# Attention into a top-1 mixture of experts: order of norms, evacuations and turned products around expert 0 and 1

## The chip, the cores and the metric

One core of a Trainium2 chip runs the whole program in one launch. The metric is the device time of an execution in microseconds. A run's profile is one more execution, taken with the hardware profiler.

## The reference

The reference is a causal attention with a learned decay (8 batches of 8 heads, 576 positions, head size 64), followed by a mixture of 8 experts over the 4608 resulting rows of 512. Each row goes to the one expert whose embedding has the largest cosine with it, and is weighted with that expert's softmax probability.

```python
scores = scale * q @ k.T + minimum(-(cum[:, None] - cum[None, :]), 0)   # causal
x = softmax(scores) @ v                       # heads side by side: 4608 x 512
logits = normalised(x) @ normalised(expert_emb).T / tau
expert_idx = argmax(logits)
out[row] = softmax(logits)[expert_idx] * (relu(x[row] @ w1[expert_idx]) @ w2[expert_idx])
```

## The kernel before

Precision is kept with pairs of 16-bit tiles, a high part and a remainder; each product of two such values is three products on the tensor engine (high by high, high by remainder, remainder by high).

**Attention.** `step(n)` (L968) is one step of a pipeline over the 64 heads, with `NH` = 64. In step n the engines do the score products and exponentials of head n, the weighted sums (`pv`, L495) of head n-2 and the norm (`norm1` to `norm3`, L515 to L541) of head n-3. All heads use one accumulator `om`, so the sums of a head wait until the norm of the head before has read it: norm of head 62, then sums of head 63. Steps 64, 65 and 66 have no new head; they finish the sums and norms of heads 62 and 63 and already start expert 0. For that, `tail(n)` (L1118) is called ahead of the sums: in steps 64 to 66 it runs `l1(0)`, `l1(1)`, `l1(2)` (L1139).

**Expert 0's first layer.** `l1(m, e, lo, hi)` (L838) computes block m of the hidden layer (128 of 1024 features) in 12 products into a buffer of PSUM, of which these blocks have two, and then evacuates it with `hsplit` (L834): ScalarE writes the relu as the high part, the vector engine subtracts it for the remainder. Blocks 3 to 7 follow after the last step (L1169).

**Weights.** They arrive by DMA in pieces of 128x512 floats. `wsq` (L790) squares a piece on ScalarE for the norm, `wnorm` (L794) turns the sums into a scale (with a small product on the tensor engine that shares `om`), `wcv` (L805) writes the high half on ScalarE and puts the remainder on a list, and `wlow` (L818) works the list off on the vector engine (L821) and lets the sync queue issue the load of a later piece. In the steps, `wcv` holds the remainders for the `wlow` of the next step (L1039). Pieces 3 and 4 of the first weights lie in the buffer that block 0's evacuated output takes.

**Routing.** When the norm of a batch's last head is done, `router` (L580) queues small vector steps (sum, maximum, comparison, one-hot `oh`, ranks). They run in `slots` and `some` (L1141). Rows are then scattered by expert in DRAM (L652) and gathered again tile by tile with `xload` (L708). `xprep(e, t)` (L725) turns a gathered tile of 128 rows around: for experts 0 and 1 with four transposes on the tensor engine, a copy on ScalarE (L750) and a subtraction on the vector engine (L752), for later experts with two transposing DMAs (L739 to L742). `xstat` (L716) takes its statistics.

**The tail.** An expert has room for 640 rows: four groups of 128, and a tail of 64 that is always computed and 64 more that run only if the expert has over 576 rows (`tc.If`, L859 and L880). The tail is computed turned around: the first layer of all eight blocks goes to one PSUM tile `T`, `l1tail` (L858) splits it, `turned` (L874) multiplies it into `yT` (12 products for a block), `l2tail` (L879) copies `yT` to SBUF on ScalarE (L884), and `l2tail_out` (L886) transposes it into `Y` and scales it out. `yT` and `Y` are the two halves of one PSUM tile (L853), a bank each, and `Y` also serves as a transposing buffer for `xprep(1, 0)` and `xprep(1, 3)`.

**Second layer.** `l2(e, t, mid)` (L901) computes group t of the output: eight times three products into one accumulator, with `mid[m]` called after block m, then `put` (L914), which scales the result on the vector engine (L917) and scatters it to the output (L918).

**The order** is written out by hand: each engine runs its instructions in the order in which the program issues them, and waits only on what it reads or overwrites.

- Expert 0's end: two rounds of tail products (L1214 to L1221), each with an `hsplit`, an `xprep` and an `xload`; then `l1tail(0)`; then `l2(0, 3)`, with `turned(0, 0)` to `turned(0, 5)` after its blocks 2 to 7, `xprep(1, 3)` and two conversions after block 1, and `xprep(1, 4)` after block 7; then `put`, two conversions, the last two turned blocks, two conversions (L1229 to L1237).
- Expert 1's end (loop over t): group 0, group 1 with its turned products, then at t = 2 the `xprep(2, 4)`, the norm, three conversions, two squares and then `l2tail(1)`; at t = 3 group 2, which calls `l2tail_out(1)` after its block 3.

Of the kernel before, what the change touches and what calls it, by code (L numbers as in the profile page):

```python
# [43 lines left out]
SPL = 384  # L44
NBIG = 1 << 20
MAIN = 512
# [63 lines left out]
def main(ctx, tc, qkh, qkc, vtin, s_in, emb, tau, w1h, w2h, out, shared, nb):  # L110
# [557 lines left out]
    X, WT, HT = {}, {}, {}  # L668
# [85 lines left out]
    def pxm():  # L754
        return ps_m.tile([128, 512], F32, tag="m", name="pxm")
# [78 lines left out]
    def hsplit(hH, hL, hp):  # L834
        nc.scalar.activation(hH, hp, AF.Relu)
        nc.vector.scalar_tensor_tensor(hL, hp, 0.0, hH, op0=ALU.max, op1=ALU.subtract)

    def l1(m, e, lo, hi, mid=None):  # L838
        h = pxs()[:, 0:hi - lo] if e else ps_t.tile([128, 2, 512], F32, tag="t", name="h")[:, 0, 0:hi - lo]
        l1mm(h, m, e, lo, hi, mid, e > 0)  # L840
        hsplit(*(t[:, lo:hi] for t in htile(m)), h)

    def four(t):
        return t.rearrange("p (m t) -> p m t", m=4)
# [78 lines left out]

    tasks, scats, mq, aq = deque(), deque(), deque(), deque()
    sent = []
    late, rq, first, placed, brk = deque(), deque(), deque(), [], [False]

    def soon(*fs):
        tasks.extendleft(reversed(fs))
# [38 lines left out]
    def step(n):  # L968
        m = n + LA - (n < 1)
        live = 0 <= n < NH  # L970
        b0, b1, c8 = n // H, n // H + 1, n % H
        prev = 0 <= n - 1 < NH
        g, c = n // HG, n % HG
        if m == 0:
            rsetup()
            load(0)
            hset(0)
            for i in range(2):
                for f in (neg, hcopy):
                    f(0, True, i)  # L980
                    f(0, False, i)
                addl(0, True, pair(i))
                addl(0, False, pair(i))
                if i == 0:
                    load(1)
                    zeros(1)
                    loadc(1)
            setup2()
            zeros(2)
        if n < 0 and rq:  # L990
            rq.popleft()()
            aq.popleft()()
            for p in range(2):
                loadt(0, pair(p))
        if m == 2:
            setup3()
        if m == 3:
            r7s[0]()
        if live and c == 0:
            hset(g + 1)  # L1000
            if n > 0:
                load(g + 2)
                loadc(g + 2)
        fslot()
        norm1(n - 3)
        if live:
            ta_(n)
        if not live or n < 2:
            s1(m)
        if n < 0:  # L1010
            heat(1)
        if prev:
            pl_(n - 1, 576, PS(n), "p")
        if n == 1:
            load(2)
        sr(m, 3)
        norm2(n - 3)
        (sa if n > 1 else s2)(m)
        if n < 0:
            heat(1)  # L1020
        if live:
            expa(n)
            if n != 1:
                prep(n, True)
        norm3(n - 3)
        if live:
            tb_(n)
        sr(m, 2)
        if n < 2:
            sr(m, 1)  # L1030
        s3(m)
        if n < 0:
            heat(2)
        if live:
            tbl(n)
        mslot()
        if prev and PS(n) < 1600:
            pl_(n - 1, PS(n), 1600, "v")
        wlow()  # L1039
        k = n - NH + 8  # L1040
        if k > 7:
            wsq((12, 14, 16)[k - 8])
        if n == 1:
            vscale(0)
            fslot()
            while tasks:
                slot()
            emm(0)
            s1(LA)
            s2(LA)  # L1050
            for i in (3, 2, 1):
                sr(LA, i)
            vcp(0, False)
            vcp(0, True)
            prep(1, True)
            s3(LA)
            emm(1)
            s4(LA)
            mrow1(LA)
        if live and n > 1:  # L1060
            emm(n)
        if n > 1:
            sb(m)
            sbr(m)
        tail(n)
        pv(n - 2, [0, 1, 2])
        if rq:
            rq.popleft()()
        if n < 2:
            s4(m)  # L1070
        if n < 0:
            heat(2)
        if n == NH - 1:
            xprep(0, 2, pxs(), False)
        pv(n - 2, [3, 4])
        if live:
            expb1(n)
            if n:
                vcp(n, False)
            else:  # L1080
                vsq(0, range(4))
        aslot()
        if n == 0:
            nc.sync.dma_start(cumd.rearrange("x r s -> r x s").bitcast(F32), chl.bitcast(F32))
            loadc(2)
            setup4()
        if live:
            prep(n, False)
            if n:
                vcp(n, True)  # L1090
        if k > 0:
            wsq((0, 2, 3, 6, 8, 8, 9, 10, 12, 14, 16)[k])
            wcv((0, 0, 0, 0, 0, 1, 2, 2, 1, 2, 0)[k], True)
        brk[0] = False
        slots(4)
        if live and 2 <= c8 < 6 and b1 < nb:
            vsq(b1, (c8 - 2,))
        if live and c8 == 6 and b1 < nb:
            vscale(b1)
        if live and c8 < 4:  # L1100
            loadt(b1, c8)
        if n == NH - 8:
            wissue(3)
        for _ in range(SCN[c8] if n < NH - 22 else 1 + (c8 > 5) + 4 * (n > NH - 6)):
            scatter()
        later()
        if live and c == (n < HG):
            addl(g + 1, True)
        if live and c == 1:
            addl(g + 1, False)  # L1110
        mrow1(m)
        if live:
            pl_(n, 0, 576, "p")
# [4 lines left out]
    def tail(n):  # L1118
        k = n - NH + 8
        if k in (2, 3):  # L1120
            wissue(7 + k % 2)
        if k == 3:
            later()
            while len(placed) < 5 * (nb - 2):
                scatter()
        if k == 4:
            HT["Kx"] = const.tile([128, 4, DM], F32, tag="KC0", name="Kx")
            HT["Qx"] = const.tile([128, 3 * XR + DM], F32, tag="QC0", name="Qx")
            wissue(16)
            xinfo(0, 0, SPL // 128)  # L1130
        if k == 5:
            wnorm()
            for t in range(3):
                xload(0, t)
        if k == 7:
            for t in range(2):
                xprep(0, t, pxs(), False)
        if 8 <= k < 11:
            l1(k - 8, 0, 0, SPL)  # L1139

    def some(k):  # L1141
        mslot()
# [23 lines left out]

    for n in range(1 - LA, NH + 3):
        step(n)
    for m in range(3, 8):  # L1169
        l1(m, 0, 0, SPL, partial(some, 12) if m == 5 else wnorm if m == 4 else None)  # L1170
        if m == 3:
            wlow()
            some(12)
        if m > 3:
            wcv((2, 1, 2, 2)[m - 4])
        if m < 6:
            xstat(0, m - 3)
        if m > 5:
            some(0)
        if m == 7:  # L1180
            for f in X[("g", 0, 0)][0:2]:
                f()
# [31 lines left out]
    for i in range(2):  # L1214
        hb = four(pxs())
        for m in range(4 * i, 4 * i + 4):
            l1mm(hb[:, m % 4], m, 0, SPL, MAIN, tail=True)
        hsplit(*(X[("T", 1)][:, k, 4 * i:4 * i + 4] for k in range(2)), hb)
        xprep(1, i, (HT["Y"], pxm())[i])
        xload(1, 3 + i)  # L1220
        gate3.popleft()()  # L1221
    l1tail(0)
    gate3.popleft()()

    def convert():
        wnorm()
        wcv(2)

    def last():  # L1229
        turned(0, 5, 0)  # L1230
        xprep(1, 4, pxm())
    mids = {m: partial(turned, 0, m - 2, 0) for m in range(2, 7)}
    l2(0, 3, {**mids, 1: lambda: (xprep(1, 3, HT["Y"]), convert()), 7: last})
    wcv(2)
    for m in (6, 7):
        turned(0, m, 0)
    wcv(2)  # L1237
    for e in range(1, NE):
        nx = e + 1 < NE
        w2, w1 = 16 * e + 8, 16 * e + 16  # L1240
        for m in range(8):
            l1(m, e, 0, MAIN)
            if e == 1 and m < 2:
                (l2tail, l2tail_out)[m](0)
            if m == 2:
# [35 lines left out]
                shared["total"] = nc.values_load(shared["ci"][0:1, NE - 1:NE], min_val=0, max_val=NT // 128)  # L1281
        l1tail(e)
        for t in range(NTL):
            if nx:
                if t + 2 < NTL:
                    xprep(e + 1, t + 2)
                if e == 1 and t < 2:
                    wsq(w1 + 6 + 2 * t)
                if t == 1 + (e == 1):
                    wnorm()  # L1290
                if t:
                    wcv(2 if e > 1 else (0, 0, 3, 3, 2)[t])
                if e > 1 or t > 1:
                    wsq(w2 + 16 + min(8, 2 * t + 2 if e > 1 else 3 * t - 4))
                if t == 4 and e > 1:
                    wnorm()
            if t == 4:
                (l2 if nx else l2h)(e, LAST)
            elif t == 3:
                l2(e, 2, {3: partial(l2tail_out, e)})  # L1300
            elif t == 2:
                l2tail(e)
            else:
                l2(e, t, tail=(t == 1))

# [123 lines left out]
```

## Time and profile before

| | |
|---|---|
| median of 3 runs | 790.51 us (788.7 to 792.61) |
| the profiled execution's own time | 788.63 us |
| span from its first to its last instruction | 786.9 us |
| tensor engine (PE) busy | 753.7 us, 96% of the span |
| vector engine (DVE) / ScalarE (ACT) / GpSimd (POOL) busy | 525.4 / 569.8 / 383.2 us |
| granted clock of the tensor engine, mean | 0.993 |

The span is the time between the first and last recorded instruction of one execution; its own time also holds the start and end around it. Times in the rows are microseconds from the span's start. A row of the timeline has start, length, engine, line, operation, output<-input, shapes and count (equal neighbours are merged, and products overlap, so lengths can reach beyond the next start); in brackets stands how long the engine was idle before it, and what released it.

### The profile page before, as it was taken

How to read it: one execution, taken by the hardware profiler on the slowest of the kernel's cores; microseconds unless marked ns; L12 is line 12 of the kernel's file. 1: busy time of each engine (PE TensorE's matmuls, PEld its weight loads, DVE VectorE, ACT ScalarE, POOL GpSimd, SP SyncE). 2: the span in 40 equal slices, each digit the busy share in tenths (PEclk: the TensorE clock that was granted, in tenths of full speed). 3: DMA queues.
4: the chain of work that ended last, by engine and by line, in shares of the span. 5: the costliest groups of instructions: out<-in, count | busy, mean ns of one | idle time of the engine just before them, and what ended most of it. 6: DMA issues, size and time to landing. Idle time of an engine off the chain costs nothing. (4 is left out here: it accounts for less than half of the span.)

```text
span 786.9 us, 22460 instructions
## 1 busy us (share of the span) xinstructions
PE 753.7 (96%) x8765; PEld 552.5 (70%) x8765; DVE 525.4 (67%) x1788; ACT 569.8 (72%) x1020; POOL 383.2 (49%) x370
## 2 busy tenths in 40 slices
PE   8799999999999999987989989999999999999997
PEld 3699999999999999984465545655645555556564
DVE  7767888888888878867656856556555566655611
ACT  6699989898999988975845876837738578475410
POOL 8767798989898979762432212130131211311001
PEclk9899999999999999999999999999999999999999
DMA  8997879797989886770634875546755857644001
GB/s 156 194 207 136 176 172 215 169 217 171 207 180 204 186 194 152 182 257 37 206 113 138 203 185 168 131 151 168 144 195 118 191 174 162 206 118 99 15 15 55
DMA packets 76914, 125.33 MB, mean 159 GB/s; under 512 B 38960, under 2 KB 39364, under 8 KB 75934
## 3 DMA queue, kind: packets, MB, share of 16 engines
q0 software_dynamic: 20240, 70.92, 38.8%
q1 hardware_dynamic: 56560, 52.84, 25.7%
q8 instruction: 76, 1.25, 0.7%
q14 instruction: 38, 0.31, 0.1%
HBM read 95.23 MB, written 21.49 MB: 148 GB/s over the span
## 5 line engine op out<-in xcount | busy, mean ns | idle before, releaser
L240 POOL TENSOR_TENSOR PL<-P 128x576 f16<-128x576 f32 (+2 forms) x128 | 203.3, 1693 | 19.5 <-ACT P L483 10.9
L830 PEld LDWEIGHTS <-wt 128*128 128x128 f16 x2016 | 114.9, 98 | 90.0 <-issue 4.6
L830 PE MATMUL pxs<-xH,wt 128*128 128x512 f16 (+1 forms) x512 | 149.8, 360 | 0.2 <-PEq L880 0.2
L918 POOL DMA_INDIRECT out<-Kx,xj x39 | 41.9, 1075 | 180.1 <-DVE Kx L917 164.5
L511 PE MATMUL om<-vh,P 128*128 128x73 f16 x960 | 106.9, 199 | 5.1 <-DVE xt L536 4.4
L512 PE MATMUL om<-vl,P 128*128 128x72 f16 x960 | 106.3, 196 | 0.0
L513 PE MATMUL om<-vh,PL 128*128 128x73 f16 x960 | 106.1, 198 | 0.0
L830 PE MATMUL T<-xH,wt 128*128 128x64 f16 x768 | 105.9, 193 | 0.0
L712 POOL DMA_INDIRECT Qx<-xs,idx x40 | 41.9, 1047 | 129.2 <-ACT vjunk L785 75.8
L348 PE MATMUL s<-qkb 96*128 96x288 f32 (+4 forms) x270 | 96.9, 372 | 2.6 <-DVE M L356 1.1
L512 PEld LDWEIGHTS <-P 128*128 128x128 bf16 x960 | 94.8, 99 | 6.2 <-issue 5.8
L513 PEld LDWEIGHTS <-PL 128*128 128x128 f16 x960 | 93.8, 98 | 0.0
L511 PEld LDWEIGHTS <-P 128*128 128x128 bf16 x960 | 93.7, 98 | 0.2
L830 PE MATMUL pxs<-xL,wt 128*128 128x512 f16 (+1 forms) x256 | 92.1, 360 | 0.0
L356 DVE CUSTOM_DVE_ANT_0 junk<-s,mS 128x320 bf16<-128x320 f32 (+3 forms) x142 | 73.2, 523 | 5.8 <-PE s L348 4.3
L905 PE MATMUL pxs<-wt,hp 128*128 128x512 f16 x270 | 73.0, 379 | 0.0
L905 PE MATMUL pxs<-wt,hq 128*128 128x512 f16 x270 | 69.4, 379 | 0.0
L486 ACT ACTIVATE P<-tb 128x1024 f32<-128x1024 f32 x64 | 65.1, 1018 | 3.2 <-PE tb L453 1.5
L917 DVE TENSOR_SCALAR Kx<-pxs,xj,idx 128x512 f32<-128x512 f32 x31 | 25.1, 808 | 59.7 <-PE pxs L905 46.2
L450 PE MATMUL tb<-QC,KC 128*128 128x448 f32 (+3 forms) x256 | 64.0, 309 | 0.0
L821 DVE SCALAR_TENSOR_TENSOR wt<-ring,idx,wt 128x512 f16<-128x512 f32 x80 | 56.9, 747 | 9.4 <-ACT wt L813 8.9
L483 ACT ACTIVATE P<-ta 128x576 f32<-128x576 f32 x64 | 41.2, 643 | 29.7 <-PE ta L450 28.0
(270 smaller groups left out, 1984.1 us busy)
## 6 DMA issues: line engine op xcount, KB each, us to landing
qkb<-qkh POOLq DMA_DIRECT2D x15, 1216.0 KB
ring<-w2h SPq DMA_DIRECT2D x44, 256.0 KB
ring<-w1h SPq DMA_DIRECT2D x36, 256.0 KB
vT<-vtin SPq DMA_DIRECT2D x28, 320.0 KB
KC<-qkh POOLq DMA_DIRECT2D x15, 576.0 KB
QC<-qkh POOLq DMA_DIRECT2D x15, 576.0 KB
rw<-w1h SPq DMA_DIRECT2D x15, 256.0 KB
rw<-w2h SPq DMA_DIRECT2D x12, 256.0 KB
```

The costliest lines, as they stand in the source:

```text
L240: nc.gpsimd.tensor_tensor(out, a, b_, op=ALU.subtract)
L348: nc.tensor.matmul(out, G[g]["QB"][0:96, h, 128 * i:128 * i + 128], G[g]["KB"][0:96, h, lo:hi], start=True, stop=True)
L356: nc.vector.tensor_tensor_reduce(out=jk, in0=src, in1=ms, scale=1.0, scalar=NEG, op0=ALU.add, op1=ALU.max, accum_out=MP[n // 2][:, n % 2, ...
L450: nc.tensor.matmul(out, HD[n]["KC"][:, ks:ks + 128], HD[n]["QC"][:, qlo:qhi], start=False, stop=stop)
L486: nc.scalar.activation(HD[n]["P32"][:, 576:1600], HD[n]["tb"], AF.Exp, scale=0.125)
L511: nc.tensor.matmul(out, lh, vh[:, kb], start=(kb == 0), stop=False)
L512: nc.tensor.matmul(out[:, u:u + 72], lh, vl[:, kb], start=False, stop=False)
L513: nc.tensor.matmul(out, ll, vh[:, kb], start=False, stop=(kb == j))
L712: ins = nc.gpsimd.indirect_dma_start(out=x.bitcast(I32), out_offset=None, in_=src, in_offset=bass.IndirectOffsetOnAxis(ap=X[("i", e, t)][1 ...
L821: nc.vector.scalar_tensor_tensor(l, a, s, h, op0=ALU.mult, op1=ALU.subtract)
L830: nc.tensor.matmul(o, w[:, 128 * c:128 * c + 128], x[:, c, a:b], start=(c == 0 and k == 0), stop=(c == 3 and k == 2))
L905: nc.tensor.matmul(y, h, w, start=a, stop=z)
```

## The change

- `l1` no longer evacuates; it returns the evacuation, and its callers run it at once, except in steps 64 to 66.
- There the evacuation is held: that of block 0 runs in step 65 and that of block 1 in step 66, each after that step's norm and after the weight remainders; that of block 2 runs after the last step. The remainders of steps 64 to 66 run in this place too (none in step 64), and no longer ahead of the norm that follows.
- In expert 0's second round of tail products, `l1tail(0)` comes before `xprep(1, 1)`, `xload(1, 4)` and a step of the gate.
- The eight turned blocks of expert 0 come two at a time after blocks 4 to 7 of `l2(0, 3)`. `xprep(1, 4)` comes after `put` and two conversions.
- For expert 1, `l2tail(1)` stands at the head of t = 2, ahead of `xprep(2, 4)`, the norm, the conversions and the squares.

```diff
     def l1(m, e, lo, hi, mid=None):
...
-        hsplit(*(t[:, lo:hi] for t in htile(m)), h)
+        return partial(hsplit, *(t[:, lo:hi] for t in htile(m)), h)
...
         norm3(n - 3)
+        if held:
+            wlow()
+            held.popleft()()
...
-        wlow()
         k = n - NH + 8
+        if k < 8:
+            wlow()
...
-            l1(k - 8, 0, 0, SPL)
+            held.append(l1(k - 8, 0, 0, SPL))
...
         step(n)
+    held.popleft()()
     for m in range(3, 8):
-        l1(m, 0, 0, SPL, partial(some, 12) if m == 5 else wnorm if m == 4 else None)
+        l1(m, 0, 0, SPL, partial(some, 12) if m == 5 else wnorm if m == 4 else None)()
...
         hsplit(*(X[("T", 1)][:, k, 4 * i:4 * i + 4] for k in range(2)), hb)
+        if i:
+            l1tail(0)
         xprep(1, i, (HT["Y"], pxm())[i])
         xload(1, 3 + i)
         gate3.popleft()()
-    l1tail(0)
     gate3.popleft()()
...
-    def last():
-        turned(0, 5, 0)
-        xprep(1, 4, pxm())
-    mids = {m: partial(turned, 0, m - 2, 0) for m in range(2, 7)}
-    l2(0, 3, {**mids, 1: lambda: (xprep(1, 3, HT["Y"]), convert()), 7: last})
+    def two(m):
+        turned(0, m, 0)
+        turned(0, m + 1, 0)
+    l2(0, 3, {1: lambda: (xprep(1, 3, HT["Y"]), convert()), **{m: partial(two, 2 * m - 8) for m in range(4, 8)}})
     wcv(2)
-    for m in (6, 7):
-        turned(0, m, 0)
+    xprep(1, 4, pxm())
     wcv(2)
...
-            l1(m, e, 0, MAIN)
+            l1(m, e, 0, MAIN)()
...
         for t in range(NTL):
+            if e == 1 and t == 2:
+                l2tail(e)
...
             elif t == 2:
-                l2tail(e)
+                if e > 1:
+                    l2tail(e)
```

## Rows read from the trace of the kernel before

**Rows 1.** Waits of the tensor engine: total us, times, longest us.
```profile
PE om L511 <- DVE xt L536: 4.4, 3, 2.5
```
**Rows 2.** Timeline of the tensor engine, 355 to 371 us.
```profile
355.33 0.19 PE L511 MATMUL om<-vh,P 128*128 128x73 f16 x1 [1.45 <-DVE xt L536]
...
356.83 0.33 PE L830 MATMUL h<-xH,wt 128*128 128x384 f16 x1
...
358.62 0.33 PE L830 MATMUL h<-xH,wt 128*128 128x384 f16 x1
361.48 0.19 PE L511 MATMUL om<-vh,P 128*128 128x73 f16 x1 [2.54 <-DVE xt L536]
...
370.73 0.18 PE L796 MATMUL om<-idx,onesb 128*128 128x8 bf16 x1 [1.03 <-DVE oh L604]
```
**Rows 3.** Timeline of the vector engine, same stretch.
```profile
355.20 2.87 DVE L493 TENSOR_TENSOR PL<-P 128x576 f16<-128x576 f32 x1
357.99 1.40 DVE L821 SCALAR_TENSOR_TENSOR wt<-vh,idx,wt 128x512 f16<-128x512 f32 x2
360.01 0.56 DVE L836 SCALAR_TENSOR_TENSOR hv<-h,hv 128x384 f16<-128x384 f32 x1 [0.62 <-ACT hv L835]
360.48 0.15 DVE L524 TENSOR_SCALAR z<-om 128x5 f32<-128x5 f32 x1
...
360.89 0.53 DVE L536 TENSOR_TENSOR xt<-om,z 128x360 f32<-128x360 f32 x1
...
369.29 0.56 DVE L836 SCALAR_TENSOR_TENSOR hp<-h,hp 128x384 f16<-128x384 f32 x1 [0.45 <-ACT hp L835]
369.76 0.20 DVE L593 TENSOR_TENSOR om<-om,rm 128x40 f32<-128x40 f32 x1
...
370.47 0.20 DVE L604 TENSOR_TENSOR oh<-wsel,om 128x40 bf16<-128x40 f32 x1
```
**Rows 4.** Timeline of ScalarE, same stretch.
```profile
359.48 0.49 ACT L835 ACTIVATE hv<-h 128x384 f16<-128x384 f32 x1 [3.82 <-DVE wt L821]
359.87 0.71 ACT L813 ACTIVATE wt<-rv,idx 128x512 f16<-128x512 f32 x1
360.48 0.62 ACT L785 ACTIVATE vjunk<-ring 128x512 bf16<-128x512 f32 x1
```
**Rows 5.** Windows: length, busy us per engine (PE, PEld, DVE, ACT, POOL), clock, DMA.
```profile
362.00:364.00 2.00, 2.00 (x38) 1.59 (x35) 1.19 (x5) 2.00 (x5) 0.00 (x0) 0.70 0.00 0
364.00:366.00 2.00, 2.00 (x7) 0.91 (x6) 1.67 (x3) 1.07 (x5) 0.00 (x0) 0.50 0.00 0
366.00:368.00 2.00, 2.00 (x13) 1.21 (x12) 0.60 (x2) 0.49 (x1) 0.00 (x0) 0.94 0.04 8
```
**Rows 6.** Timeline of the tensor engine, end of expert 0, 408 to 420 us.
```profile
408.84 0.81 PE L905 MATMUL pxs<-wt,xH 128*128 128x512 f16 x3
412.08 0.51 PE L877 MATMUL yT<-xH,wt 128*128 128x64 f16 x12 [2.43 <-DVE xL L752]
...
419.45 0.19 PE L830 MATMUL T<-xL,wt 128*128 128x64 f16 x1 [0.24 <-DVE xL L752]
```
**Rows 7.** Timeline of the vector engine, 409 to 420 us.
```profile
409.21 1.23 DVE L836 SCALAR_TENSOR_TENSOR xH<-T,xH 128x1024 f16<-128x1024 f32 x1 [0.34 <-ACT xH L835]
...
411.35 0.68 DVE L752 TENSOR_TENSOR xL<-yT,xH 128x512 f16<-128x512 f32 x1
...
418.70 0.69 DVE L752 TENSOR_TENSOR xL<-pxm,xH 128x512 f16<-128x512 f32 x1 [3.52 <-ACT xH L750]
419.31 0.80 DVE L917 TENSOR_SCALAR Kx<-pxs,xj,idx 128x512 f32<-128x512 f32 x1
```
**Rows 8.** Timeline of the tensor engine, end of expert 1.
```profile
463.13 0.66 PE L889 MATMUL yT<-ident,Kx 128*128 128x128 f32 x4 [2.99 <-ACT Kx L884]
```
**Rows 9.** Timeline of ScalarE, end of expert 1.
```profile
454.62 0.62 ACT L739 CAST xr<-Qx 128x512 f16<-128x512 f32 x1 [0.66 <-DMA xH<-xr]
...
462.51 0.56 ACT L884 COPY Kx<-yT 128x512 f32<-128x512 f32 x1
```

More of the change, by code (lines that the diff above doesn't have):

```diff
@@ L925, in main @@
     sent = []
-    late, rq, first, placed, brk = deque(), deque(), deque(), [], [False]
+    late, rq, first, placed, brk, held = deque(), deque(), deque(), [], [False], deque()
     def soon(*fs):
```

## The prediction

> **What bounds the kernel now.** I read the page's busy shares first: the tensor engine is busy for 96% of the span, so a change can win only the microseconds in which that engine waits, or runs at half clock. Next came its waits. Three weighted sums `om` wait for a normalised head `xt`, 4.4 us together, the longest 2.5 us [rows 1]. Then I went to the places that the diff touches, in order of time, with a few lines per engine. The tensor engine stands still there four times: 2.54 us ahead of the sums of head 63 and 1.03 us ahead of the weights' norm product [rows 2]; 2.43 us ahead of the first turned product of expert 0 [rows 6]; 2.99 us ahead of the tail's transposes of expert 1 [rows 8]. A fifth wait, 1.45 us ahead of the sums of head 62 [rows 2], lies before anything that the change moves, and stays. A row's length has some 0.16 us of drain at its end: blocks of 12 products, each 0.33 long, start 0.163 us apart ((358.62-356.83)/11) [rows 2].
>
> **The joint (steps 64 to 66).** Today, once head 63's leftover subtraction is done (355.20 plus 2.87, so 358.07), the vector engine does two weight remainders (1.40 us), waits 0.62 us, splits block 0 (0.56), and only then takes the norm of head 62, from 360.48 to 361.42 [rows 3]. The wait is for ScalarE's relu of block 0, which itself waited for the second remainder [rows 4], since they share a buffer. The tensor engine was through with block 1 at 358.95 and idles until 361.48 [rows 2]. The change puts the norm first: it then runs from about 358.0 to 358.95, and the sums of head 63 start at 359.0 in place of 361.48, that is 2.5 us sooner. They take 1.5 us, as those of head 62 did (355.33 to 356.83) [rows 2], to 360.5.
>
> What is late next are the held evacuations, for the blocks have two buffers. Three remainders (0.70 each) now follow the norm, to 361.0, then the split of block 0, to 361.5. Its relu fits in after the second remainder. Block 2 needs that buffer, and starts at 361.5: a new wait of 0.9 us. Block 2 takes 12 x 0.163 + 0.16 = 2.1 us. On ScalarE the relu of block 0 (0.49) is followed by two squares (0.74 apart with their readout), two conversions (0.71 each, the second overlapping) and the relu of block 1 [rows 4]: 360.3 + 0.5 + 1.5 + 1.3 + 0.5 gives about 364.0, and its split ends at 364.7. So block 3 starts at 364.7, a second new wait of over 1 us, and ends at 366.8. Relu and split of block 3 take 1.05 us, then the five router steps from 369.76 to 370.67 take 0.91 us [rows 3], and the norm product that waits for the last of them comes at 368.85 where it came at 370.73. That is 1.9 us of gain, though 2.5 were removed; I take 1.8. Behind this product the router, the scatters, the gathers and their consumers follow in the order they have now, so I let them move along. The remainders also release weight loads on the sync queue, about 1 us later, for weights of expert 1, which are converted only during expert 0's last group: nothing. Bounds: 0.2, if the clock drops once more in the new waits, and 2.5, if the whole stall goes.
>
> [...] It fell right after the 2.54 us stall and came back under steady products. With shorter, more evenly spread waits I expect no fall; if it falls, block 2 or 3 takes up to twice its 1.95 us, and the gain is near 0.6.
>
> **The tail of expert 0.** The first turned product now waits for the subtraction of the fourth gathered tile (411.35 plus 0.68, so 412.03; products from 412.08), not for the tail's split, which was done at 410.44 [rows 6, 7]. The subtraction reads `Y`, the other half of the tile whose first half the turned products write. The change brings the split forward, but the vector engine does the same work before that subtraction in another order, and its only idle moment there is 0.34 us [rows 7]; so the subtraction still ends near 411.95. The tensor engine gets there two groups of three later: 408.84 plus 3 x 0.65 is 410.8 (0.81 less 0.16 each) [rows 6]. The stall is 1.2 us in place of 2.43. Then eight turned groups (0.35 each) and three groups of three make 4.75 us, to 416.7.
>
> What is late next is on the vector engine: the output's scaling (0.80) can start when the last group of three ends, near 416.2, and the change queues it and two remainders (1.40) ahead of the fifth tile's statistics (about 0.3) and its subtraction (0.69) [rows 3, 7]. That sums to 419.4, and expert 1's first layer needs this subtraction at its fourth product, which came at 419.45 [rows 6]. Gain: 0.1 us. The wait is shifted, not removed. Bounds: 0.7 lost, if those remainders or the transposes' round trip come later than that, and 1.3 won, if the products do not wait for `Y`.
>
> [...] The row of 412.08 disagrees: the engine resumed 0.05 us after the subtraction and 1.6 us after the split.
>
> **The copy of expert 1.** The copy of `yT` (0.56 us) runs at 462.51 on ScalarE behind the next expert's row copies, three conversions and two squares, and the transposes wait for it until 463.13 [rows 8, 9]. With the change it stands ahead of all of them and runs when the turned products end. The transposes are due at 460.1 (463.13 less 2.99), the turned products end just ahead of the four groups of three (0.65 each) before that, near 457.4, so the copy is done by 458.0 and the stall goes whole: 2.99 us. Behind the moved copy, ScalarE's row copy of expert 2's fifth tile slips from 454.62 [rows 9] to 458.0, and with it that tile's two transposing DMAs on the sync queue, the norm and the conversions, by up to 3 us for the first and about 1 us for the rest. Expert 2 needs the tile after the transposes (0.5) and twelve more groups of three (7.8), at 463.1 + 8.3 = 471.4 today and 468.4 then, some 10 us after its row copy: covered, and if that cover were gone each microsecond would come back as a wait of its first layer. Bounds: 2.0, if a later scaling holds a buffer, and 3.1.
>
> The If's skip, the DMAs and the count of instructions are the same; I cost them at nothing.
>
> **Sum.** 1.8 + 0.1 + 3.0 = 4.9 us against the profiled execution's own 788.63 (span 786.9): 783.7. The median of the runs shown is 790.51, 1.9 above that execution; I forecast 790.51 - 4.9 = 785.6.
>
> **The rivals.**
> - *The turned products wait for the split alone.* Then expert 0 gives 1.3, the sum is 6.1, the time 784.4. For it: the buffer halves are disjoint. Against it: the row above. 0.17.
> - *The joint gives back what it saves.* The new waits of blocks 2 and 3 (0.9 and 1.2) grow, or the clock falls there as it does today, or the scatters behind are set by their own landing; the joint gives 0, the sum is 3.1, the time 787.4, inside 0.5%. For it: two blocks in a row now wait for a held split, and the clock did fall in this stretch. 0.23.
> - *The copy's stall moves.* Expert 2's first layer waits for the later fifth tile or for a buffer, 1.5 us or more come back; the sum is about 3.2, the time 787.3. Against it: 10 us of cover. 0.05.
> - *Slower: the clock stays down.* Place: blocks 2 to 7 after the joint. Waits of 1.45, 0.9, 1.2 and 1.1 us now stand close together; if the granted clock stays at 0.50 through all six blocks, each costs 1.95 us more, 11.7 in all, and the time is 790.5 - 4.9 + 11.7 = 797.3. It decides from about four and a half blocks on ((4.9 + 3.95)/1.95). Against it: today it fell after a wait of 2.54 and returned within 3.4 us [rows 5], and no wait here is that long. 0.05. [...]
>
> **How the numbers follow.** The forecast as worked out has 0.50. A measurement of this kernel can tell about 0.5%, 3.95 us. The forecast case spreads over sums of 3.2 to 5.9, nine tenths of it beyond 3.95; with the first rival that makes 0.62 for faster. The rest of the forecast, the second and third rival make 0.33 for the same, and the last 0.05 for slower. The range takes the sums of the bounds, 0.2 - 0.7 + 2.0 = 1.5 and 2.5 + 1.3 + 3.1 = 6.9, off the median: 783.6 to 789.0, widened by 0.4 downwards because the runs of before alone lie 3.9 apart.
>
> **What would show it.** Right: the sums of head 63 within 0.1 us after block 1; blocks 2 and 3 each with a wait of about 1 us for a split; the norm product some 2 us sooner; the first turned product behind `L752` with about 1.2 us of wait and a second wait of over 1 us at expert 1's first layer; no wait ahead of expert 1's transposes. Wrong: granted clock of 0.50 beyond 366 us; turned products that start without a wait; a new wait at expert 2's first layer; or waits of blocks 2 and 3 that add up to over 4 us.

## The result, and the profile after

The changed kernel takes 782.72 us in the median of 6 runs (780.62 to 784.78), the kernel before 789.55 (6 runs, 787.88 to 792.61): ratio 0.9909, 95% interval 0.9883 to 0.9934. That is a gain of 7.2 us by the ratio and 6.8 by the two medians, where 4.9 were forecast. The time lies 0.5 us below the range. Three more comparisons followed, each on a chip of its own: 0.9947 (0.9927 to 0.9968), 0.9922 (0.9900 to 0.9944) and 0.9943 (0.9923 to 0.9963). All four together, weighted by the inverse squares of their half-widths, give 0.9933 (0.9922 to 0.9944), which is 5.3 us of the 788.2 that 75 executions of the kernel before have as their median.

The profiled execution of after took 780.62 us (span 778.5). Its tensor engine around the joint:

```profile
353.13 0.20 PE L511 MATMUL om<-vh,P 128*128 128x73 f16 x1 [0.72 <-DVE xt L536]
...
359.26 0.32 PE L830 MATMUL h<-xH,wt 128*128 128x384 f16 x1 [0.81 <-DVE hv L836]
362.56 0.32 PE L830 MATMUL h<-xH,wt 128*128 128x384 f16 x1 [1.19 <-DVE hp L836]
366.67 0.18 PE L796 MATMUL om<-idx,onesb 128*128 128x8 bf16 x1 [1.03 <-DVE oh L604]
...
406.93 0.86 PE L877 MATMUL yT<-xH,wt 128*128 128x64 f16 x24 [0.71 <-DVE xL L752]
412.98 0.19 PE L830 MATMUL T<-xH,wt 128*128 128x64 f16 x1 [0.46 <-ACT xH L750]
414.28 0.19 PE L830 MATMUL T<-xL,wt 128*128 128x64 f16 x1 [0.89 <-DVE xL L752]
...
454.91 0.60 PE L889 MATMUL yT<-ident,Kx 128*128 128x128 f32 x4
```

Against [rows 2], the 2.54 us ahead of the sums of head 63 are gone, and blocks 2 and 3 wait 0.81 and 1.19 us for held splits. Against [rows 6], 0.71 us stand ahead of the turned products in place of 2.43, and 0.46 and 0.89 come at expert 1's first layer. Against [rows 8], expert 1's transposes wait for nothing. The wait ahead of the sums of head 62 is 0.72 us, not 1.45, though nothing ahead of it was moved. The windows from 358 to 366 us show no half clock, where [rows 5] had 0.70 and 0.50:

```profile
358.00:360.00 2.00, 1.19 (x19) 0.83 (x16) 1.93 (x6) 1.84 (x6) 0.00 (x0) 1.00 0.00 0
360.00:362.00 2.00, 1.37 (x9) 0.69 (x8) 1.45 (x4) 2.00 (x5) 0.00 (x0) 1.00 0.00 0
362.00:364.00 2.00, 1.44 (x9) 0.87 (x9) 1.76 (x5) 1.50 (x6) 0.00 (x0) 1.00 0.05 8
364.00:366.00 2.00, 1.64 (x11) 0.78 (x8) 0.89 (x4) 1.10 (x3) 0.00 (x0) 1.00 0.00 0
```

On ScalarE the copy now runs as soon as the turned products end, ahead of the row copy that stood before it in [rows 9]:

```profile
452.27 0.58 ACT L884 COPY Kx<-yT 128x512 f32<-128x512 f32 x1 [3.29 <-PEq L880]
452.76 0.62 ACT L739 CAST xr<-Qx 128x512 f16<-128x512 f32 x1
```

So every wait went where the prediction sent it. Open were the sizes. The two profiles also differ by 1.5 us that had gathered by the first of the weights' norm products (338.45 us before, 336.94 after), and by the 0.7 us at head 62; the change cannot have made either.

### The profile page after: what moved, and what is told of

Its sections match the earlier page's. It is cut to its first block, busy times and chain, and to the rows that moved or that the text cites. A ratio compares the mean times of both kernels' runs of the same rounds, so it can differ in the third digit from the quotient of the medians.

```text
span 778.5 us, 22464 instructions
## 1 busy us (share of the span) xinstructions
PE 752.4 (97%) x8765; PEld 552.4 (71%) x8765; DVE 525.3 (67%) x1788; ACT 569.8 (73%) x1020; POOL 382.2 (49%) x370
```

## The experiments

**One part alone** (one chip). joint_only, tail_only and copy_only are the kernel before with one part of the diff each; before_again is that kernel unchanged. Of each edit the heart:

```diff
 joint_only:
+        if held:
+            wlow()
+            held.popleft()()
...
 tail_only:
+        if i:
+            l1tail(0)
...
+    l2(0, 3, {1: lambda: (xprep(1, 3, HT["Y"]), convert()), **{m: partial(two, 2 * m - 8) for m in range(4, 8)}})
...
 copy_only:
+            if e == 1 and t == 2:
+                l2tail(e)
```

> The kernel before with the joint's part of the change alone (norm of head 62 and 63 ahead of the weight remainders and the evacuations of blocks 0 to 2). Theory A, the prediction's step: the norm product of the weights at the router comes 1.9 us earlier counted from the sums of head 62, nothing else moves, ratio 0.9977 (1.8 of 789.5). Theory B, the 0.7 us ahead of the sums of head 62 and the 0.83 us at the fourth gathered tile's transposes are effects of the joint too: both waits short here as in the changed kernel, 1.8 + 0.7 + 0.8 = 3.3 us, ratio 0.996. Theory C, those two waits differ between executions whatever the kernel: they may be long or short here and in the kernel before run again alike.

> The kernel before with the part on expert 0's tail alone (its split sooner, turned products in pairs in the last four groups, fifth tile's preparation behind the scaling). The prediction's step: first turned product behind the fourth tile's subtraction with a wait of 1.2 us in place of 2.43, a second wait of over 1 us at expert 1's first layer, together 0.1 us, ratio 0.9999. What the changed kernel's trace shows would be 0.3 us (waits of 0.7, 0.5 and 0.9 where 2.4 and 0.2 stood), ratio 0.9996. Rival (products wait for the split alone): no wait ahead of the turned products, 1.3 us, ratio 0.9984. The waits of the joint (2.5) and of expert 1's transposes (3.0) stay in every theory.

> The kernel before with the part on expert 1's copy alone (its turned products' copy at the head of the third tile's turn, ahead of row copies, conversions and squares). The prediction's step: the wait of 2.99 us ahead of expert 1's transposes goes whole, no new wait at expert 2's first layer, 3.0 us, ratio 0.9962. Rival (the stall moves): 1.5 us or more come back at expert 2's first layer or at a buffer, ratio 0.998 or above.

> The kernel before, unchanged, profiled a second time. If the waits of 1.45 us (sums of head 62) and 0.83 us (fourth tile's transposes) belong to the kernel's order, both stand here within 0.1 us, as do those of 2.54, 2.43 and 2.99 us. If they vary between executions, one or both differ here by some 0.5 us with no edit, and the span with them; the start of the stretch (the same instruction near 304 us) would then also differ by a microsecond or more, as it does between the first profile of before and that of the changed kernel.

Measured: joint_only 786.9 us, ratio 0.9994 (0.9968 to 1.0021); tail_only 786.61, 0.9998 (0.9980 to 1.0017); copy_only 783.32, 0.9956 (0.9931 to 0.9981). So the copy is worth 3.5 us (1.5 to 5.4), the tail 0.2, and of the joint's 1.8 only 0.5 shows, within an interval that holds both.

The profile of before_again bears out theory C for the wait ahead of head 62: with no edit, its 1.45 us are gone there. The 0.83 us of the gathered tile is 0.67 there, and in before_third no such wait stands. And it shows what the first profile did not. Its tensor engine at the two later stalls, and the windows behind them (the third column from the end is the clock):

```profile
409.42 0.51 PE L877 MATMUL yT<-xH,wt 128*128 128x64 f16 x12 [2.43 <-DVE xL L752]
...
461.90 1.11 PE L889 MATMUL yT<-ident,Kx 128*128 128x128 f32 x4 [2.99 <-ACT Kx L884]
```

```profile
408.00:410.00 2.00, 0.58 (x14) 0.46 (x14) 1.83 (x11) 0.00 (x0) 0.00 (x0) 1.00 0.56 149
410.00:412.00 2.00, 2.00 (x18) 1.17 (x17) 1.36 (x3) 1.95 (x4) 0.00 (x0) 0.62 0.00 0
412.00:414.00 2.00, 2.00 (x17) 1.08 (x15) 0.52 (x4) 0.00 (x0) 0.00 (x0) 0.52 0.65 192
...
460.00:462.00 2.00, 0.10 (x1) 0.10 (x2) 0.90 (x2) 1.97 (x7) 0.00 (x0) 0.92 0.64 196
462.00:464.00 2.00, 2.00 (x7) 1.20 (x8) 1.50 (x3) 2.00 (x4) 0.00 (x0) 0.50 0.58 198
464.00:466.00 2.00, 2.00 (x8) 0.84 (x7) 1.30 (x2) 1.94 (x7) 0.42 (x1) 0.72 0.75 255
```

Behind the stalls of 2.43 and 2.99 us the granted clock fell, to 0.62 and 0.52 behind the first and to 0.50 and 0.72 behind the second, which cost another 1.6 us each (21.4 and 18.9 us between the norm products around them, where the first profile of before has 19.8 and 17.3). In that first profile the clock stood at 1.00 behind both:

```profile
412.00:414.00 2.00, 1.92 (x30) 1.28 (x30) 1.26 (x7) 1.30 (x3) 0.00 (x0) 1.00 0.05 16
...
464.00:466.00 2.00, 2.00 (x11) 0.88 (x9) 2.00 (x4) 1.97 (x5) 0.00 (x0) 1.00 0.45 159
```

The same waits thus cost different sums in different executions.

**The changed kernel again, less a part, and with two repairs** (another chip). after_again is the change itself; no_tail has the tail as before; the other two edit the changed kernel:

```diff
 pool_first:
...
+        if n == NH - 2:
+            pl_(n, 0, 576, "p")
+            pl_(n, 576, PS(n + 1), "p")
         for _ in range(SCN[c8] if n < NH - 22 else 1 + (c8 > 5) + 4 * (n > NH - 6)):
             scatter()
...
-        if live:
+        if live and n != NH - 2:
...
 tail_free:
-        xprep(1, i, (HT["Y"], pxm())[i])
+        xprep(1, i, HT["Y"])
...
-    l2(0, 3, {1: lambda: (xprep(1, 3, HT["Y"]), convert()), **{m: partial(two, 2 * m - 8) for m in range(4, 8)}})
+    l2(0, 3, {1: lambda: (xprep(1, 3, pxm()), convert()), **{m: partial(two, 2 * m - 8) for m in range(4, 7)}, 7: lambda: (xprep(1, 4, pxm()), two(6))})
     wcv(2)
-    xprep(1, 4, pxm())
```

> The changed kernel, unchanged, in more executions beside the kernel before. The profiles taken so far put 1.8 us on the joint (end of head 63's leftover subtraction to the router's last step: 12.3 to 12.4 us without the change, 10.6 with it), 0.4 on expert 0's tail and 3.2 on expert 1's copy: 5.4 us, ratio 0.9931. Theory C (clock): the removed stalls of 2.4 to 3.0 us also cost clock in a part of the executions (0.50 after the first stall in every profile that has it, after the second or third in two of four), so the mean granted clock here is above that of the kernel before (0.990) by 0.002 to 0.004, and the gain is 6.5 to 8 us, ratio 0.990 to 0.992. Theory S (scatter of the runs alone): same clock as before, ratio 0.993.

> The changed kernel with expert 0's tail put back as it was (joint and copy changed alone), so the 2.43 us wait ahead of the first turned product stands again. By the waits alone it loses 0.4 us against the changed kernel (2.4 and 0.2 where 0.7, 0.5 and 0.9 stand). Theory C: in a part of the executions the granted clock falls to 0.50 after that wait, which costs another 1.5 us there, so the median is 0.4 to 1.9 us above the changed kernel's and the mean clock a little lower. Theory S: 0.4 us, same clock.

> The changed kernel with GpSimd's two leftover subtractions of head 62 issued ahead of the five scatters that they follow today (GpSimd idles for 3.9 us ahead of those). Theory P: head 63's leftover subtraction on VectorE, 0.75 us for every other head but 2.9 to 4.9 here, ends 0.6 us after GpSimd's last subtraction in all six profiles, because it waits for GpSimd; with two of four subtractions (2.0 us) gone from behind the scatters it ends up to 2 us sooner, the norm of head 62 follows, and the router's last step comes 1 to 2 us sooner, counted from the sums of head 61 (20.8 us in the profile of the joint alone). Ratio to before 0.002 below the changed kernel's. Rival: the subtraction is long for a reason of its own or the sums of head 62 set the end; then its end stays where it is against the sums of head 61, and the time is that of the changed kernel.

> The changed kernel with expert 1's second tile transposed into Y and its fourth into the other buffer (so the last reader of Y comes two microseconds sooner), and its fifth tile prepared ahead of the last pair of turned products. If the turned products wait for Y's reader (the prediction's step), their wait of 0.7 us goes; if they wait for the split of the tail, which ends 2.5 us sooner, or for their own inputs, it stays. The waits of 0.5 and 0.9 us at expert 1's first layer go with the earlier fifth tile. Together up to 2.1 us against the changed kernel, 0.0026 of the time; if its gathered rows land too late for the earlier place, a new wait ahead of its transposes takes a part back.

Measured: after_again 783.92, 0.9947 (0.9927 to 0.9968); no_tail 784.7, 0.9968 (0.9952 to 0.9984); pool_first 783.86, 0.9945 (0.9924 to 0.9966); tail_free 780.87, 0.9913 (0.9893 to 0.9934). The time of after_again spoke for theory S, its mean clock of 0.993 against 0.991 for theory C. In no_tail the clock fell behind the 2.43 us once more, to 0.56 and 0.58 in two windows of 2 us.

tail_free gains 2.2 us from the third to the fourth of the weights' norm products (17.2 against 19.3; the later expectation that calls them second and third counts from zero), and its turned products start without a wait:

```profile
411.23 0.86 PE L877 MATMUL yT<-xH,wt 128*128 128x64 f16 x24
412.58 0.86 PE L877 MATMUL yT<-xH,wt 128*128 128x64 f16 x24
...
417.27 0.19 PE L830 MATMUL T<-xL,wt 128*128 128x64 f16 x1 [0.24 <-DVE xL L752]
```

All that moved for them is the last reader of `Y`. The fourth tile's subtraction, which no longer reads `Y`, still ends at 412.06, after the products have begun:

```profile
411.38 0.68 DVE L752 TENSOR_TENSOR xL<-pxm,xH 128x512 f16<-128x512 f32 x1
```

So in the changed kernel they wait for the reader of the other half of their tile, and not for the tail's split: an engine waits here on more than the "what it reads or overwrites" of the kernel's order. The prediction's step had it so. The wait of 0.71 us in after ends on a signal of the subtraction, so it is an order that the program keeps, and no run here shows whether the hardware needs it.

pool_first turned up what the joint's first row really is. In the profiles of before and of before_again the leftover subtraction's seven rows have these lengths (ns, minimum, median, maximum):

```profile
L493 DVE TENSOR_TENSOR PL<-P x7: 746/748/2868, 324.6 to 355.2; 128x576 f16<-128x576 f32 x7
```

```profile
L493 DVE TENSOR_TENSOR PL<-P x7: 748/748/4226, 323.3 to 351.4; 128x576 f16<-128x576 f32 x7
```

Five take 0.75 us and one, which also begins beside a GpSimd subtraction, 1.57; the one of head 63 is the longest, and it ends 0.6 us after the last of GpSimd's four subtractions (here of before_again: 351.44 + 4.23 against 350.99 + 4.06), whatever its own start:

```profile
351.44 4.23 DVE L493 TENSOR_TENSOR PL<-P 128x576 f16<-128x576 f32 x1
```

```profile
350.99 4.06 POOL L240 TENSOR_TENSOR PL<-P 128x576 f16<-128x576 f32 x4
```

With two of the four gone from there it took 1.05 us in pool_first and the router's last step came 0.9 us sooner, counted from the sums of head 61; the norm of head 62 then waited 0.78 us for the sums themselves. Theory P holds, its price is half of what was expected, and the time does not show it. In the twelve profiles where the row takes 2.8 us or more, it ends behind all four GpSimd instructions (4.04 to 4.06 us together), and in joint_only and copy_only VectorE's row begins 0.2 us first and ends last. That GpSimd's subtractions make the wait is shown by pool_first; in what way they make it is not.

**The total, the joint and a best version** (two more chips). after_third and after_fourth are the changed kernel, before_third the kernel before, tail_free_2 a repeat. all3 is tail_free with pool_first's edit. best2 is all3 with the following, with the squares of steps 65 and 66 later in their step, and with the transposes of `third` and `fourth` behind groups 3 and 6; no_joint and no_joint_free are the changed kernel and tail_free without the joint's hunks.

```diff
 best2:
-            held.append(l1(k - 8, 0, 0, SPL))
+            f = l1(k - 8, 0, 0, SPL)
+            held.append(f) if k == 8 else f()
...
-        l1(m, 0, 0, SPL, partial(some, 12) if m == 5 else wnorm if m == 4 else None)()
+        l1(m, 0, 0, SPL, partial(some, 12) if m == 5 else None)()
+        if m == 4:
+            wnorm()
```

> The changed kernel once more beside the kernel before, since two comparisons so far gave 0.9909 (0.9883 to 0.9934) and 0.9947 (0.9927 to 0.9968). Their mean, weighted by the widths, is 0.993. Theory W (waits alone): the three parts as measured in traces, 1.8 + 0.4 + 3.2 = 5.4 us, ratio 0.9931. Theory C (clock besides): 0.5 to 2 us more, for half-clock stretches behind the 2.4 and 3.0 us waits in about half of the executions of the kernel before, ratio 0.991 to 0.9925. Below 0.991 or above 0.996 neither holds.

> The kernel before, unchanged, profiled beside these. From the sums of head 61 to those of head 62 the profiles gave 7.2 us (first profile of before), 5.2 (four kernels in the first call) and 6.6 (the changed kernel and the four of the second call). If this belongs to the chip or the placement and not to the change, it is the same here as in the three kernels that run beside it. The joint from the end of head 63's leftover subtraction to the router's last step takes 12.3 to 12.4 us, whatever that distance is. Half clock after the 2.5 us wait as in every profile that has it; after the waits of 2.4 and 3.0 us it may or may not fall.

> The changed kernel with both improvements that the traces bear out: GpSimd's two subtractions of head 62 ahead of the scatters (0.9 us at the router, of which the gather's landing may take 0.6 back) and the freed Y with the earlier fifth tile (2.2 us). Sum 2.5 to 3.1 us against the changed kernel in the same runs, 0.003 to 0.004 of the time. If the two share a cover (the later gather delays the tiles), only 2.2.

> The kernel of all3 with three more moves: only block 0's evacuation is held, blocks 1 and 2 evacuate in their own step with the squares behind them on ScalarE; the weights' norm product comes behind block 4 and not inside it; the gathered fourth and fifth tiles of expert 0 are transposed two groups later. Theory B: blocks 2 and 3 wait for evacuations that ScalarE does behind two squares and two conversions (0.8 and 1.2 us today), so the router's last step comes up to 1.2 us sooner; the norm product's 1.0 us goes; the gather's landing then is the bound, and the two later groups (1.3 us at 0.65 each for the full size, less for these) hide it. 1 to 2.5 us against all3. Rival: the norm of head 63, now behind block 1's split, or the gather takes all of it back: the time of all3.

> The changed kernel without the joint's part (tail and copy changed alone). Theory J (the joint is worth its 1.8 us in every execution): 1.8 us slower than the changed kernel beside it, ratio to before 0.9954 where that has 0.993. Theory L (it depends on how late the sums of head 61 are): a difference between 0 and 1.8, and the profile shows 12.3 to 12.4 us from the end of head 63's leftover subtraction to the router's last step where that subtraction is long (it waits for GpSimd), about 10.8 where it takes 0.75 us.

> The changed kernel beside the one without the joint. Ratio to before 0.993 (mean of three comparisons, 0.9916 to 0.9942). In the profile: where head 63's leftover subtraction is long, 10.6 us from its end to the router's last step; where it takes 0.75 us, the norm of head 62 waits for the sums of head 62, two remainders and block 0's evacuation stand behind that wait, and it is 12 to 13 us (theory L); theory J has 10.6 in both cases.

> The changed kernel with the freed Y and the earlier fifth tile, once more: 2.2 us below the changed kernel by its profile (from the second to the third of the weights' norm products 17.2 us where the changed kernel has 19.3), ratio to before 0.990.

> The same without the joint's part. Theory J: 1.8 us slower than tail_free_2, ratio 0.9925. Theory L: equal to it or up to 1.8 us slower, by the share of executions in which TensorE is late at the sums of head 61.

Measured: after_third 783.41, 0.9922 (0.9900 to 0.9944); all3 782.72, 0.9902 (0.9876 to 0.9929); best2 784.4, 0.9932 (0.9908 to 0.9956); no_joint 784.18, 0.9935 (0.9913 to 0.9957); after_fourth 784.16, 0.9943 (0.9923 to 0.9963); tail_free_2 780.94, 0.9906 (0.9871 to 0.9941); no_joint_free 781.29, 0.9909 (0.9882 to 0.9936).

Without the joint's part the kernel is not told from the one with it, twice: 784.18 beside 784.16, 781.29 beside 780.94. Theory J falls by the profiles, which also say why. The length of head 63's subtraction (L493), and the time from its end to the start of the router's last step (L604):

| without the joint | L493 | to L604 | with the joint | L493 | to L604 |
|---|---|---|---|---|---|
| before | 2.87 | 12.40 | after | 2.85 | 10.57 |
| before_again | 4.23 | 12.32 | joint_only | 4.88 | 10.58 |
| tail_only | 4.23 | 12.37 | after_again | 2.86 | 10.58 |
| copy_only | 4.88 | 12.34 | no_tail | 2.83 | 10.57 |
| no_joint | 2.81 | 12.19 | tail_free | 2.83 | 10.58 |
| no_joint_free | 2.84 | 12.39 | tail_free_2 | 2.89 | 10.58 |
| before_third | 0.75 | 10.76 | after_fourth | 1.94 | 11.96 |
| | | | after_third | 0.75 | 13.14 |

In six profiles of each kind the joint gives 1.8 us, as worked out. In the others TensorE came late to block 0 and so to the sums of head 62, the subtraction waited less or not at all for GpSimd, and the norm that the change puts first waits for the sums (all3 is another such profile, with 0.75 and 12.90). VectorE in after_third:

```profile
356.50 0.75 DVE L493 TENSOR_TENSOR PL<-P 128x576 f16<-128x576 f32 x1
359.72 0.17 DVE L524 TENSOR_SCALAR z<-om 128x5 f32<-128x5 f32 x1 [2.48 <-PE om L513]
```

Three remainders and the split of block 0 stand behind those 2.48 us, where the order of before does them meanwhile (before_third, 10.76). Theory L holds in its mechanism; the share of such executions is not known from 15 profiles. By the three timed differences (0.5 us for it alone, 0.0 and 0.3 for the two pairs, each good to some 2 us) no gain is shown; taken together they leave room for about 1 us, and not for the full 1.8.

Part of that lateness is clock. In after_fourth the tensor engine idles for 1.81 us ahead of block 0, and the granted clock is 0.50 from 354 to 356 us, inside that block, whose products then start 0.32 us apart in place of 0.16:

```profile
352.09 0.32 PE L830 MATMUL h<-xH,wt 128*128 128x384 f16 x1 [1.81 <-issue]
```

```profile
354.00:356.00 2.00, 2.00 (x8) 0.92 (x7) 1.95 (x3) 1.97 (x5) 2.00 (x4) 0.50 0.33 129
```

In after_third and all3 the granted clock is 0.50 in the window from 356 to 358 us; in before_third, which idles for 1.84 us there, it stays at 1.00. So the 2.4 us between after_third and before_third are not the order's alone. The rest stays open: in all 18 profiles block 0 starts 0.05 to 0.12 us after ScalarE's copy of the third gathered tile, and the profile does not show why that copy, or in before_third the tile's transposes, come late.

all3 does not beat tail_free by time, and best2, whose profile is the shortest of all (span 776.9, router 1.7 us sooner than in pool_first), had four of six executions at a clock of 0.991 or less; neither is told from the other. tail_free beats both kernels: it is 3.0 us below the changed kernel beside it, and 3.2 below when repeated (0.9906).

**What the two later stalls cost.** From the third to the sixth of the weights' norm products, by the tensor engine's rows, the four profiles that have both stalls take 65.5 us (before), 68.5 (before_again), 68.2 (joint_only) and 67.1 (before_third), the mean being 67.3. The granted clock fell behind the 2.99 us stall in three of these four, to 0.50, and behind the 2.43 in one, to 0.52. With the profiles that have one of the two stalls (tail_only, copy_only, no_tail) it is three of five and two of six. The six with both parts changed and `Y` as in the change (after, after_again, after_third, after_fourth, pool_first, no_joint) take 61.9 to 62.0, and with `Y` freed 59.7 to 59.9 (tail_free, tail_free_2, no_joint_free, all3, best2). Without a fall the two parts are worth 3.6 us, tail_only 0.6 and copy_only 3.4 by the same measure; with the falls 5.4 in the mean. The times do not tell these two apart: no_joint gains 5.1 us (3.4 to 6.9), tail_only and copy_only 3.7 together. The granted clock goes the same way, though unevenly: 0.9898 in the mean of 75 executions of before, 0.9925 in 28 of after; 0.9897 with the joint alone, 0.9921 in no_joint, 0.9905 in no_joint_free. Within the 75 the time goes down as the clock goes up (correlation -0.65).

## Why the prediction was right and wrong

**Direction and mechanism: right.** Each wait went, shrank or appeared where it was put: 0.81 and 1.19 at blocks 2 and 3 for the 0.9 and over 1 forecast, the turned products behind `L752`, a second wait at expert 1's first layer (0.46 + 0.89 for over 1), none at expert 1's transposes and none new at expert 2's. The gain over four comparisons, 5.3 us (4.4 to 6.1), is near the 4.9, and part of that is luck: of the joint's 1.8 us the times show 0 to about 1, and the tail and the copy gave 3.7 (tail_only and copy_only) to 5.1 us (no_joint) where 3.1 were forecast. The time of the first, 782.72, is not in the range.

**The step that failed: the base of the range.** "Off the median" is off the 790.51 us of three runs. The six runs beside the changed kernel put the same program at 789.55, and 75 more in the later comparisons at 788.2. Of the 2.9 us between the forecast of 785.6 and the 782.72, 1.0 is this base and 1.9 is gain. The gain of 6.8 us by the medians is still inside the sum of the bounds, 6.9; laid off 789.55 the same range would have begun at 782.2 and held the result. Three runs that lie 3.9 us apart needed more than the 0.4 us by which the range was widened.

**The term left out: the clock, in the bounds of the tail and the copy.** These bounds end at the length of the wait ("Bounds: 2.0 ... and 3.1", "1.3 won"), and the range's lower end is built from them. The stalls of 2.43 and 2.99 us also cost clock in part of the executions (granted 0.50 to 0.56 at the lowest behind five of the eleven that the profiles hold), 1.8 us in the mean of four profiles for the two stalls; how much of that the times contain is not shown. The one profile read had a fall behind the joint's stall alone [rows 5], so the prediction priced clock only there, although waits of the same length stood at [rows 6] and [rows 8].

**The tail, 0.1.** Waits alone gave 0.6. The subtraction of the fourth tile ended 2.79 us behind the third norm product, where the working had it 3.14 and the kernel before 3.22, so the first wait is 0.71 and not 1.2.

**The copy, 3.0.** Right: 3.4 by itself, 3.5 by time (1.5 to 5.4). Its 10 us of cover held: no new wait of expert 2's first layer.

**The joint, 1.8.** Right to the tenth in twelve profiles (12.35 less 10.58), wrong as an average. The step took 2.87 as the subtraction's length; five sisters of 0.75 said that the row holds a wait. And "it then runs from about 358.0" left out that a norm put first can itself wait, with ready work behind it: the rival "The joint gives back what it saves" is near what the times show, by another way than it named. The way that it did name, the scatters' landing, does not show: from the router's norm product to the next one the profiles take 37.4 to 38.8 us with the joint and 37.6 to 38.5 without.

**"A fifth wait ... stays."** It was 1.45, 0.72 or nothing with the same code; a wait seen in one profile was taken as the kernel's.

**The rivals.** The turned products do not wait for the split: the 0.71 us in after end on `L752`, and in tail_free, where the last reader of `Y` comes sooner, they start without a wait. The clock did not stay down behind the joint's new waits: it stands at 1.00 there in the six profiles whose windows show them (after, joint_only, after_third, after_fourth, all3, tail_free_2).

## What to carry to other kernels

Price a long TensorE stall at its length and, in part of the executions, the lower clock behind it, even where the one profile at hand has none (here 0.50 to 0.56 at the lowest behind five of eleven stalls of 2.43 or 2.99 us, worth 1.6 us each in before_again). Take the base of a forecast from as many runs as their spread asks for: here three runs were 2.3 us off the median of 75, half of the gain in question. A row much longer than its sisters of the same line and shape can hold a wait (here 2.8 to 4.9 us against 0.75); look for the engine that ends just before it (GpSimd, 0.6 us). On an engine that works in order, moving a step that waits ahead of steps that are ready pays only as long as its input is in time (here 10.58 us to the router's last step where it was, 11.96 to 13.14 where it was not), so ask how much that input moves between executions.

## What was unexpected of the hardware

VectorE's subtraction of 0.75 us took 2.8 to 4.9 us beside GpSimd's four in twelve profiles and ended 0.6 us after them, even where its row begins 0.2 us before theirs (joint_only: 351.26 against 351.47). And the same instructions, ahead of anything that the change moves, let the sums of head 62 wait 0 to 1.45 us, and TensorE idle up to 1.8 us around the third gathered tile, for a cause that the profile does not show.
